# Sums of phi(k) times v in two 64-column halves of the matmul array, two tiles' sums together

## The chip, the cores and the metric

The kernel runs on one core of a Trainium2 chip. The metric is the device time of one execution in microseconds; lower is better. TensorE (PE) multiplies, VectorE (DVE), ScalarE (ACT) and GpSimd (POOL) do the work element by element, and SyncE (SP) issues most DMAs. PEld is the loading of the weights (the stationary operand) of a matmul, which has rows of its own in the profile.

## The reference

```python
# x: (1, 2048, 576); xn = layernorm(x); H = 32 heads of Dh = 18 columns
q, k, v = split(xn @ wqkv)                       # per head
phi = lambda t: jnp.where(t > 0, t + 1, jnp.exp(t)) + 1e-6
pq, pk = phi(q), phi(k)
kv  = einsum("bhsd,bhse->bhde", pk, v)           # the sums: 18 x 18 per head, over all 2048 rows
z   = einsum("bhsd->bhd", pk)
num = einsum("bhqd,bhde->bhqe", pq, kv)
den = einsum("bhqd,bhd->bhq", pq, z)[..., None] + 1e-6
s = (num / den) @ wo
g = silu((gelu(xn @ w_gate) * (xn @ w_up)) @ w_down)   # 576 -> 4608 -> 576
out = x + s * g
```

The change is in `kv` and `z` alone. A head's sum needs only that head's 18 columns of phi(k) against its own 18 columns of v.

## The kernel before

The 2048 rows are 16 tiles of 128 rows (t = 0 to 15). The first part of the program (to about 283 us) makes q, k and v, the sums, and the attention output s; the rest (gate, up and down products with a fast matrix multiplication in blocks) takes the remaining 1180 us and does not change.

**A tile.** `kv_tile(t)` makes k and v of one tile in three products: `x_mm(t, 0)` gives 416 columns of k, `x_mm(t, 1)` the last 160 of k and 252 of v, `x_mm(t, 2)` the last 324 of v and 64 of q. Each is 14 matmuls with operands in fp32r, into one bank of PSUM (`kv_<t>_<c>` in the program; the profile leaves the numbers out and calls all of them `kv`). After `x_mm(t, 0)`, PE broadcasts the next tile's mean and scale (`turn`, tile `ms`; for the first four tiles it transposes x, tile `xt`). DVE forms phi(k) in `pk` (`k_post`: `e_k` and `pk` are its two halves, then ACT takes exp and POOL adds), ACT copies v into `va` (`v_post`), and DVE and ACT normalize and place the next tile (`place`: `x<-x,ms`, `xf_B`, `xo_B`), which the next `x_mm(t + 1, 0)` reads. At the end of each even tile from 2 to 12 DVE takes the moments of two later tiles (`x_next`: `bn`, `mv`, `st`), which a later `turn` broadcasts. All instructions of an engine stand in the order in which the code is written.

**The sums.** `kv_mm(t)` adds tile t's share into PSUM. The 32 heads are five groups: four of 7 heads (126 columns) and one of 4 (72 columns). For each group one fp32 matmul has `va` of the group as weights (a column of ones for z, then 126 or 72 columns of v) and `pk` of the group as the moving operand, so that all 7 x 7 pairs of heads are computed, and the 18 x 18 blocks on the diagonal are cut out by a mask at the end. The groups of 7 lie in the bank `kv_a`, the last in `kv_b`. An fp32 matmul is two matmul instructions and two weight loads in the profile: 4 groups give 8 rows of `kv_a`, the last gives 2 of `kv_b`. `kv_mm(t - 1)` stands in `kv_tile(t)` after `x_mm(t, 2)`; the sums of tiles 0 and 1 stand in tile 2's hand-written code, those of tile 7 and 15 behind the first product of q (`q_store(0, 0)`, `q_hold(2, 7, 0)`). Tile 8 has none.

**Buffers.** `pk` and `va` come from one ring of four (`slot`), so `pk[t]` takes the buffer of `pk[t - 2]`.

**What follows.** `kv_done` multiplies both banks by the mask into `kvm` (DVE). `kv_wo` multiplies `kvm` with the matching rows of `wo` (PE, tile `kw`) into weights that the output product needs. `load_wo` clears row 0 and some columns of `wo_t` and `kvm` on POOL and loads `wo` by DMA. `den` computes the denominators: 5 groups of 4 fp32 matmuls with 32 columns of weights each, the four on the four quarters of the output's partitions (tile `d`).

Of the kernel before, what the change touches and what calls it, by code (L numbers as in the profile page):

```python
# [8 lines left out]
F32 = mybir.dt.float32  # L9
F32R = mybir.dt.float32r  # L10
BF16 = mybir.dt.bfloat16
AF = mybir.ActivationFunctionType
ALU = mybir.AluOpType
# [3 lines left out]
P = 128  # L17
S = 2048
# [12 lines left out]
NHG = 5  # L31
WIDTHS = [GW, GW, GW, GW, D - 4 * GW]
W4 = WIDTHS[4]


Q4 = 64
# [54 lines left out]
def block_kernel(ctx, tc, x, xe, xt, wq_d, wkv_d, wo, wgu_d, wd_d, out):  # L91
# [9 lines left out]
    def own_bank(name):  # L101
        return ps.tile([P, 512], F32, tag="own", bufs=2, name=name)
# [7 lines left out]
    def slot(shape, dt, name):  # L110
        return sb.tile(shape, dt, tag="h", bufs=4, name=name)
# [9 lines left out]
    def act(*args, **kw):  # L121
        pin(nc.scalar.activation(*args, **kw))  # L122

    def vec(op, *args, **kw):
        pin(getattr(nc.vector, op)(*args, **kw))  # L125

    def mm(*args, **kw):
        pin(nc.tensor.matmul(*args, **kw))  # L128

    def pool(op, *args, **kw):  # L130
        pin(getattr(nc.gpsimd, op)(*args, **kw))  # L131

    def dma(out, in_, eng=None):
        tc.keep_in_program_order((eng or nc.sync).dma_start(out=out, in_=in_))
# [156 lines left out]
    def difference(s, i):  # L291
        f = xf[s]
        nm, a, b, o = SUMS[i]
        vec("tensor_sub", f[o], f[a], f[b])
        f[nm] = f[o]
# [81 lines left out]

    acc = []

    def kv_out(gi):  # L380
        return acc[0][:, gi * P : (gi + 1) * P] if gi < 4 else acc[1][:, 0:P]

    def phi(o, src, name):

# [5 lines left out]

    def kv_mm(t):
        if t == 0:
            acc.extend(own_bank(n) for n in ("kv_a", "kv_b"))
        pk, va = pks.pop(t), vas.pop(t)
        for gi, wdt in enumerate(WIDTHS):
            mm(
                kv_out(gi)[0 : wdt + 1, 0:wdt],
                va[:, gi, 0 : wdt + 1], pk[:, gi * GW : gi * GW + wdt],
                start=(t == 0 and gi in (0, 4)), stop=(t == S // P - 1),
                skip_group_check=True,  # L400
            )


    KV_PASSES = [(0, 0), (1, 1), (3, 0), (4, 1), (0, 3), (1, 4), (2, 2)]
# [5 lines left out]
    def x_mm(t, c, js=(0, 1), passes=KV_PASSES):  # L410

        tb, i = divmod(t, TT)
        s, b = divmod(tb, 2)
        begin = (t, c) not in pkv
        if begin:
            pkv[t, c] = bank(f"kv_{t}_{c}")
        o = pkv[t, c]
        for j in js:
            for n, (wi, xi) in enumerate(passes):
                mm(  # L420
                    o[:, 0 : TW[c]], xo[s][BS[b][j]][:, xi, i * P : (i + 1) * P], kv_part(c, j, wi),
                    start=(begin and j == 0 and n == 0), stop=(j == 1 and (wi, xi) == (2, 2)),
                )
# [33 lines left out]
    def v_post(t, c):  # L457

        if c == 1:
            vas[t] = slot([P, NHG, P], F32, f"va_{t}")  # L460
            pool("memset", vas[t][:, :, 0:1], 1.0)
        va, src = vas[t], pkv[t, c]
        n = D - TW[0] if c == 1 else 0
        g = 2 * c - 2
        act(
            va[:, g : g + 2, 1 : GW + 1],
            src[:, n : n + 2 * GW].rearrange("p (g j) -> p g j", g=2), AF.Copy,
        )
        if c == 2:
            act(va[:, 4, 1 : W4 + 1], src[:, 2 * GW : 2 * GW + W4], AF.Copy)  # L470
            tb, i = divmod(t, TT)
            if i == 0:
                qt[tb] = gl_tile([P, TT, 2, Q4], f"qt_{tb}")
            act(
                qt[tb][:, i], src[:, None, 2 * GW + W4 : TW[2]].to_broadcast([P, 2, Q4]), AF.Copy,
            )
# [5 lines left out]
    def kv_tile(t, mid_=(), end=()):  # L482

        ahead = t % (2 * TT) != 2 * TT - 1
        x_mm(t, 0)
        if ahead:
            turn(t + 1)
        k_post(t, 0)
        x_mm(t, 1)
        if ahead:  # L490
            place(t + 1)
            save(t + 1)
        run(list(mid_))
        k_post(t, 1)
        v_post(t, 1)
        x_mm(t, 2)
        if t - 1 in vas:
            kv_mm(t - 1)
        run(list(end))
        v_post(t, 2)  # L500

    ph, ph_d = {}, {}

# [48 lines left out]
    def make_masks():  # L552
        ones = tmp([P, NHG * H], "ones")
        nc.gpsimd.memset(ones, 1.0)

        at["mask"] = mask = small[:, 0:GW]
        m3, o3 = (i.rearrange("p (h j) -> p h j", h=HG) for i in (mask, ones[:, 0:GW]))
        nc.gpsimd.affine_select(
            out=m3, in_=o3, compare_op=ALU.is_ge, fill=0.0, base=-1,
            pattern=[[-DH, HG], [0, DH]], channel_multiplier=1,  # L560
        )
        nc.gpsimd.affine_select(
            out=m3, in_=m3, compare_op=ALU.is_ge, fill=0.0, base=DH,
            pattern=[[DH, HG], [0, DH]], channel_multiplier=-1,
        )
        nc.gpsimd.memset(mask[0:1, :], 1.0)
        at["maskh"] = small[:, P : P + NHG * H].rearrange("p (g h) -> p g h", g=NHG)
        band(at["maskh"], ones.rearrange("p (g h) -> p g h", g=NHG), [[-GW, NHG], [DH, H]], 1)
        at["zc"] = small[:, P + NHG * H : P + 2 * NHG * H].rearrange("p (g h) -> p g h", g=NHG)
        nc.gpsimd.memset(at["zc"][Q4:P], 0.0)  # L570

    def kv_done():

        mask, kvm = at["mask"], at["kvm"]
        n, n4 = GW + 1, W4 + 1
        vec("tensor_mul", kvm[0:n4, 4, 0:W4], acc[1][0:n4, 0:W4], mask[0:n4, 0:W4])
        vec(
            "tensor_mul", kvm[0:n, 0:4, 0:GW],
            acc[0][0:n, :].rearrange("p (g j) -> p g j", g=4)[:, :, 0:GW],
            mask[0:n, None, :].to_broadcast([n, 4, GW]),  # L580
        )

    def load_wo():

        n = NHG * P
        t = big(14, [P, n + D + 2], F32, "kvm")
        at["kvm"] = t[:, 0:n].rearrange("p (g j) -> p g j", g=NHG)
        at["wo"] = w = big(12, [P, 4, D + 2], F32, "wo_t")
        at["wo4"] = w4 = t[:, n:]
        for t in (w, w4[:, None, :]):  # L590
            pool("memset", t[0:1, :, 0:D], 0.0)
            pool("memset", t[:, :, D:], 0.0)
            pool("memset", t[0:1, :, D : D + 1], 1.0)
        dma(out=w[1 : GW + 1, :, 0:D], in_=wo[0 : 4 * GW, :].rearrange("(g p) e -> p g e", p=GW))
        dma(out=w4[1 : W4 + 1, 0:D], in_=wo[4 * GW : D, :])

    def kv_wo(gi):

        if gi == 4:
            at["kvh"] = big(4, [P, 4, D], F32R, "kvh")  # L600
            at["kvl"] = big(5, [P, 4, D], F32R, "kvl")

            at["kv4"] = big(6, [P, 4, D], F32R, "kv4")
            pool("memset", at["kv4"][Q4:P, 1, :].bitcast(F32), 0.0)
        kvh, kvl, kv4 = at["kvh"], at["kvl"], at["kv4"]
        zc, mh = at["zc"], at["maskh"]
        wdt, k = (W4, W4 + 1) if gi == 4 else (GW, GW + 1)
        w = at["wo4"] if gi == 4 else at["wo"][:, gi]
        pw = []
        for c, cs in enumerate((slice(0, HALF), slice(HALF, D + 2))):  # L610
            pw.append(bank(f"kw_{gi}_{c}"))
            mm(
                pw[c][0:wdt, 0 : cs.stop - cs.start], at["kvm"][0:k, gi, 0:wdt], w[0:k, cs],
                start=True, stop=True,
            )
        r, x_ = slice(0, Q4 if gi == 4 else GW), slice(Q4, W4)
        z = pw[1][:, HALF : HALF + 1]

        def parts(hi, lo, rows):
            for c in range(2):  # L620
                cs = slice(c * HALF, (c + 1) * HALF)
                split(hi[:, cs], lo[:, cs], pw[c][rows, 0:HALF])

        if gi == 4:
            vec("tensor_copy", zx[x_], z[x_])
            parts(kv4[x_, 2, :], kv4[x_, 3, :], x_)
            for c in range(2):
                act(kv4[Q4:P, 0, c * HALF : (c + 1) * HALF], pw[c][r, 0:HALF], AF.Copy)

        vec(  # L630
            "tensor_scalar", zc[r, gi, :], mh[r, gi, :], z[r], None, op0=ALU.mult,
        )
        if gi == 4:
            parts(kv4[r, 0, :], kv4[r, 1, :], r)
        else:
            parts(kvh[r, gi, :], kvl[r, gi, :], r)
# [754 lines left out]
    for passes in (HI_X, LO_X):  # L1391
        for j in range(2):
            x_mm(2, 0, (j,), passes)
    kv_mm(0)
    turn(3)
    k_post(2, 0)
    x_mm(2, 1)
# [3 lines left out]
    k_post(2, 1)  # L1401
    v_post(2, 1)
    x_mm(2, 2)
    kv_mm(1)
    x_next(4)
    v_post(2, 2)
    load_q(0)
# [27 lines left out]
    def form_apart(nm):  # L1435
# [11 lines left out]
        dma(out=d[:, 2], in_=last[:, 0].bitcast(F32))  # L1447

    behind = {
        (0, 0): [lambda: kv_mm(N0 - 1), lambda: spread(N0, 2), lambda: difference(0, 3)],  # L1450
        (0, 1): [
            lambda: scales(N0), lambda: form("T1"), lambda: q_store(1, 4),
        ],
# [9 lines left out]
    for n in range(N0, 2 * N0):  # L1463
# [12 lines left out]
        if n in (N0, N0 + 2):  # L1476
            load_x(n + 4, 2)
    ahead = {
        (2, 0): [lambda: kv_mm(2 * N0 - 1), kv_done, spread_sel, lambda: difference(1, 3)],
        (2, 1): [lambda: kv_wo(4), lambda: q_hold(2, 7, 4)],  # L1480
        (2, 2): [lambda: kv_wo(0), lambda: kv_wo(1), move_rows],
        (2, 3): [lambda: kv_wo(2), lambda: kv_wo(3)],
# [118 lines left out]
```

## Time and profile before

| | before |
|---|---|
| time, median of 3 runs | 1461.74 us (1460.86 to 1463.02) |
| the profiled execution | 1461.7 us, span 1460.0 us |
| granted TensorE clock | 1.00 |
| PE busy | 1452.8 us, 100% of the span |
| DVE busy | 1154.8 us, 79% |
| `kv_a` matmuls | 128 rows, 16.7 us busy |
| `kv_b` matmuls | 32 rows, 4.7 us busy |

The profiled execution took 1.7 us more than its span. A row of the timeline gives the start in us from the span's beginning, the length in us, the engine, the line, the operation, the tiles (written <- read), the sizes, and how many instructions are merged; brackets hold the idle time of the engine before it and what ended it. A matmul's length contains the way through the array, so that matmuls in a row overlap: the step from start to start is what one costs.

### The profile page before, as it was taken

Reading aid. Unit: us, or ns where it says so; the run is one execution under the profiler, and the core shown is the slowest. Engines: PE = TensorE matmul, PEld = TensorE weight load, DVE = VectorE, ACT = ScalarE, POOL = GpSimd, SP = SyncE. Lnnn points to the kernel's source line nnn. Section 1 sums busy time; section 2 is a strip of 40 time slices with the busy share of each in tenths; the row PEclk is TensorE's granted clock in tenths of the full one; section 3 lists DMA queues with packets and bytes.
Section 4 is the critical chain, followed back from the end, with each engine's and each line's share of the span. In section 5 each row is a group of like instructions: output and inputs, shape, how many; then the busy total and the mean of one; then the engine's idle time right before and its main releaser. Section 6 shows DMA issues by size and latency. Waiting matters only on the chain.

```text
span 1460.0 us, 21848 instructions
## 1 busy us (share of the span) xinstructions
PE 1452.8 (100%) x8126; PEld 1297.1 (89%) x8126; DVE 1154.8 (79%) x1603; ACT 561.5 (38%) x914; POOL 577.9 (40%) x512
## 2 busy tenths in 40 slices
PE   9999999999999999999999999999999999999998
PEld 8989989988888888888888888888889999999998
DVE  7687676376888787878778878778788978989888
ACT  6344265333222332322333222322335556555454
POOL 3342340125665567565575664657632000000000
PEclk9999999999999999999999999999999999999999
DMA  6445006531333315323152242323379888767886
GB/s 228 164 188 194 6 2 214 192 144 57 124 123 115 129 58 174 101 94 130 61 178 87 94 152 84 133 87 106 130 268 354 268 259 250 251 187 234 276 291 223
DMA packets 118068, 233.96 MB, mean 160 GB/s; under 512 B 11002, under 2 KB 44666, under 8 KB 116042
## 3 DMA queue, kind: packets, MB, share of 16 engines
q1 hardware_dynamic: 115162, 220.31, 45.0%
q0 software_dynamic: 2656, 12.06, 2.2%
q8 instruction: 64, 1.05, 0.3%
q14 instruction: 42, 0.34, 0.1%
q10 hardware_dynamic: 144, 0.20, 0.0%
HBM read 149.91 MB, written 82.58 MB: 159 GB/s over the span
## 4 chain that ended last, share of the span: by engine, by line
PE 97%; DVE 2%; ACT 0%; issue 0%; DMA 0%; DVEq 0%; ACTq 0%
PE bd L128 25%; PE ga L818 16%; PE de L818 16%; PE al L818 16%; PE be L818 8%; PE kv L128 8%; PE s L128 4%; PE q L128 4%; PE kv_a L128 1%; PE d L128 0%; PE kw L128 0%; PE b L128 0%; DMA x<-in_xe_dram 0%; DVE acc L125 0%; PE xt L221 0%
## 5 line engine op out<-in xcount | busy, mean ns | idle before, releaser
L131 POOL TENSOR_TENSOR sm<-raw 128x384 f32<-128x384 f32 x72 | 75.5, 1049 | 148.8 <-DMA raw<-in_wgu_dram 113.8
L128 PE MATMUL kv<-wkv,xo_B 128*128 128x412 f32 (+2 forms) x662 | 128.0, 349 | 0.0
L125 DVE TENSOR_TENSOR wa<-sm,wa 128x768 fp32r<-128x768 f32 x72 | 94.7, 1315 | 36.1 <-ACT wa L122 35.3
L128 PEld LDWEIGHTS kv<-wkv,xo_B 128*128 128x128 f32 x662 | 119.6, 188 | 1.0 <-ACT xo_B L122 0.2
L128 PE MATMUL bd<-w_head,hi 128*128 128x288 f32 x516 | 117.9, 294 | 0.0
L125 DVE TENSOR_TENSOR wb<-raw,wb 128x256 fp32r<-128x256 f32 (+1 forms) x108 | 103.9, 962 | 7.4 <-ACT wb L122 5.8
L125 DVE TENSOR_TENSOR wa<-raw,wa 128x256 fp32r<-128x256 f32 x72 | 68.7, 955 | 51.0 <-ACT wa L122 47.7
L122 ACT ACTIVATE hi<-raw_h 128x1024 fp32r<-128x1024 f32 x59 | 62.4, 1060 | 94.2 <-PE bd L128 60.8
L128 PE MATMUL bd<-w_end,hi 128*128 128x288 f32 x448 | 89.8, 294 | 0.0
L122 ACT ACTIVATE spot_h<-spot_h 128x512 f32<-128x512 f32 x49 | 30.8, 633 | 152.0 <-DVE spot_h L125 152.0
L128 PEld LDWEIGHTS bd<-w_head,hi 128*128 128x128 f32 x516 | 87.0, 188 | 0.1
L125 DVE TENSOR_TENSOR raw_h<-raw_h,hi 128x1024 fp32r<-128x1024 f32 x59 | 71.7, 1219 | 18.5 <-ACT hi L122 18.5
L128 PE MATMUL bd<-w_end,raw_h 128*128 128x288 f32 x264 | 77.9, 295 | 0.0
L122 ACT ACTIVATE wa<-sm 128x1152 fp32r<-128x1152 f32 x36 | 41.8, 1161 | 88.5 <-PE de L818 86.3
L122 ACT ACTIVATE u<-al 128x512 f32<-128x512 f32 x72 | 41.0, 593 | 89.7 <-PE al L818 69.0
L128 PEld LDWEIGHTS bd<-w_end,hi 128*128 128x128 f32 x448 | 71.9, 188 | 0.0
L128 PE MATMUL bd<-beside,raw_h 128*128 128x288 f32 x240 | 70.8, 295 | 0.0
L131 POOL TENSOR_TENSOR spot_h<-spot_h,spot_h 128x512 f32<-128x512 f32 x45 | 62.8, 1401 | 2.9 <-DVE spot_h L125 2.4
L818 PE MATMUL ga<-xo_B,wb 128*128 128x512 f32 x252 | 63.1, 390 | 0.4 <-DVE u L125 0.4
L818 PE MATMUL al<-xo_B,wa 128*128 128x512 f32 x252 | 63.0, 389 | 0.0
L818 PE MATMUL al<-xr_B,wa 128*128 128x512 f32 x252 | 63.0, 389 | 0.0
L818 PE MATMUL be<-xr_T,wa 128*128 128x512 f32 x252 | 63.0, 389 | 0.0
(274 smaller groups left out, 4055.1 us busy)
## 6 DMA issues: line engine op xcount, KB each, us to landing
raw_h<-hs SPq DMA_DIRECT2D x176, 256.0 KB
raw<-in_wgu_dram SPq DMA_DIRECT2D x36, 768.0 KB
hs<-spot_h SPq DMA_DIRECT2D x90, 256.0 KB
hs<-spot_g SPq DMA_DIRECT2D x80, 256.0 KB
b<-in_wd_dram SPq DMA_DIRECT2D x42, 432.0 KB
hs<-spot_m SPq DMA_DIRECT2D x38, 256.0 KB
raw_g<-hs SPq DMA_DIRECT2D x22, 256.0 KB
raw_a<-hs SPq DMA_DIRECT2D x20, 256.0 KB
```

Source lines behind the costliest of these rows:

```text
L122: pin(nc.scalar.activation(*args, **kw))
L125: pin(getattr(nc.vector, op)(*args, **kw))
L128: pin(nc.tensor.matmul(*args, **kw))
L131: pin(getattr(nc.gpsimd, op)(*args, **kw))
L818: nc.tensor.matmul(o, w[0:rows, wi, :], xop[0:rows, xi, :], start=(start and n == 0), stop=(n == len(PASSES) - 1), skip_group_check=True,)
```

## The change

Each group is now two matmuls on two halves of the array's columns. The first half has the ones and the group's first 63 columns of v (3.5 heads) as weights and writes to partitions 0 to 63, the second the ones and the other 63 to partitions 64 to 127. The middle head is split between them. Against each go only the 4 heads of phi(k) that its half touches (72 columns instead of 126). The group of 4 heads becomes two halves of 37 weights and 36 moving columns. All lie in the one bank `kv_a`. `va` has ten pieces of 64 columns instead of five of 128. And the sums of two tiles are made one after the other: `kv_pair(t)` stands in even tiles behind `x_mm(t, 0)`, ahead of `turn`, and makes tiles t - 2 and t - 1; the pairs for 6 and 7, and for 14 and 15, stand behind the first product of q.

```diff
+KC = 4 * DH
-    def kv_out(gi):
-        return acc[0][:, gi * P : (gi + 1) * P] if gi < 4 else acc[1][:, 0:P]
+    def kv_out(gi, half):
+        n, m = (KC, GW // 2) if gi < 4 else (W4 // 2, W4 // 2)
+        c = half * ((GW if gi < 4 else W4) - n)
+        r = half * P // 2
+        return acc[0][r : r + m + 1, gi * KC : gi * KC + n], slice(c, c + n)
...
         for gi, wdt in enumerate(WIDTHS):
-            mm(
-                kv_out(gi)[0 : wdt + 1, 0:wdt],
-                va[:, gi, 0 : wdt + 1], pk[:, gi * GW : gi * GW + wdt],
-                start=(t == 0 and gi in (0, 4)), stop=(t == S // P - 1),
+            for half in range(2):
+                o, cs = kv_out(gi, half)
+                mm(
+                    o, va[:, 2 * gi + half, 0 : o.shape[0]],
+                    pk[:, gi * GW + cs.start : gi * GW + cs.stop],
+                    start=(t == 0 and gi == 0), stop=(t == S // P - 1),
...
 def v_post(t, c):
-            va[:, g : g + 2, 1 : GW + 1],
-            src[:, n : n + 2 * GW].rearrange("p (g j) -> p g j", g=2), AF.Copy,
+            va[:, g : g + 4, 1 : GW // 2 + 1],
+            src[:, n : n + 2 * GW].rearrange("p (g j) -> p g j", g=4), AF.Copy,
...
 def kv_tile(t, mid_=(), end=()):
         x_mm(t, 0)
+        if t % 2 == 0:
+            kv_pair(t)
         if ahead:
             turn(t + 1)
...
         x_mm(t, 2)
-        if t - 1 in vas:
-            kv_mm(t - 1)
+    def kv_pair(t):
+        for i in (t - 2, t - 1):
+            if i in vas:
+                kv_mm(i)
...
 def kv_done():          # two multiplications by a mask become four, two for each half
-        vec("tensor_mul", kvm[0:n4, 4, 0:W4], acc[1][0:n4, 0:W4], mask[0:n4, 0:W4])
+            vec("tensor_mul", kvm[r, 4, cs], o, mask[r, 0 : W4 // 2])
+            vec(
+                "tensor_mul", kvm[r, 0:4, cs],
+                acc[0][r, 0 : 4 * KC].rearrange("p (g j) -> p g j", g=4),
+                at["mask"][r, None, :].to_broadcast([P // 2, 4, KC]),
+            )
...
 def load_wo():          # wo's rows lie in two halves too; what no row covers is zero
+        pool("memset", at["kvm"], 0.0)
         for t in (w, w4[:, None, :]):
-            pool("memset", t[0:1, :, 0:D], 0.0)
-            pool("memset", t[:, :, D:], 0.0)
-            pool("memset", t[0:1, :, D : D + 1], 1.0)
-        dma(out=w[1 : GW + 1, :, 0:D], in_=wo[0 : 4 * GW, :].rearrange("(g p) e -> p g e", p=GW))
-        dma(out=w4[1 : W4 + 1, 0:D], in_=wo[4 * GW : D, :])
+            pool("memset", t, 0.0)
+            for r in (0, P // 2):
+                pool("memset", t[r : r + 1, :, D : D + 1], 1.0)
+        for half in range(2):
+            r = half * P // 2 + 1
...
+            dma(out=w[r : r + n, :, 0:D], in_=rows[:, half])
...
+            dma(out=w4[r : r + n, 0:D], in_=wo[f : f + n, :])
```

`make_masks` builds the masks of the two halves in six steps on POOL instead of two, with four short memsets instead of one, and `kv_wo` sums over 128 and 101 rows instead of 127 and 73.

The order on PE around tile 10, where `pk_1193` and `va_1225` belong to tile 8 and `pk_1268` and `va_1300` to tile 9; first as it stood before, from the last matmul of tile 9's products to the broadcast for tile 11:

```order
L128 MATMUL kv_2_1303<-wkv_73,xo_B_1079 128x388
L128 MATMUL kv_a<-pk_1193,va_1225 127x126 x4
L128 MATMUL kv_b<-pk_1193,va_1225 73x72
L128 MATMUL kv_0_1332<-wkv_71,xo_B_1076 128x416 x7
L128 MATMUL kv_0_1332<-wkv_72,xo_B_1079 128x416 x7
L213 MATMUL ms_1347<-ident,mv_1117 128x128
L213 MATMUL ms_1347<-ident,st_1124 128x128
L128 MATMUL kv_1_1354<-wkv_73,xo_B_1076 128x412 x7
```

The same place now (the buffers of tiles 8 and 9 are `pk_1239`, `va_1271` and `pk_1314`, `va_1346`):

```order
L129 MATMUL kv_2_1349<-wkv_73,xo_B_1125 128x388
L129 MATMUL kv_0_1373<-wkv_71,xo_B_1122 128x416 x7
L129 MATMUL kv_0_1373<-wkv_72,xo_B_1125 128x416 x7
L129 MATMUL kv_a<-pk_1239,va_1271 64x72 x8
L129 MATMUL kv_a<-pk_1239,va_1271 37x36 x2
L129 MATMUL kv_a<-pk_1314,va_1346 64x72 x8
L129 MATMUL kv_a<-pk_1314,va_1346 37x36 x2
L214 MATMUL ms_1408<-ident,mv_1163 128x128
L214 MATMUL ms_1408<-ident,st_1170 128x128
```

The sum of tile 8 has moved behind the first product of tile 10, that of tile 9 from behind tile 10's last product to the same place, and the broadcast `ms` for tile 11 comes behind both.

On POOL at the end of tile 13 stood, between the last addition of phi(k) of that tile and the next, these rows of `load_wo`:

```order
L131 TENSOR_TENSOR pk_1616<-pk_1616,e_k_1617 128x576
L131 MEMSET va_1648 128x5
L131 MEMSET wo_t 1x4x576
L131 MEMSET wo_t 128x4x2
L131 MEMSET wo_t 1x4
L131 MEMSET kvm 1x576
L131 MEMSET kvm 128x2
L131 MEMSET kvm 1x1
L131 TENSOR_TENSOR pk_1702<-pk_1702,e_k_1703 128x576
```

Now there stand:

```order
L132 TENSOR_TENSOR pk_1682<-pk_1682,e_k_1683 128x576
L132 MEMSET va_1714 128x10
L132 MEMSET kvm 128x640
L132 MEMSET wo_t 128x2312
L132 MEMSET wo_t 1x4 x2
L132 MEMSET kvm 128x578
L132 MEMSET kvm 1x1 x2
L132 TENSOR_TENSOR pk_1786<-pk_1786,e_k_1787 128x576
```

The memsets clear whole tiles instead of one row and two columns, and the DMAs that fill `wo_t` and `kvm` write over what they cleared.

More of the change, by code (lines that the diff above doesn't have):

```diff
@@ L392, in kv_mm @@
         if t == 0:
-            acc.extend(own_bank(n) for n in ("kv_a", "kv_b"))
+            acc.append(own_bank("kv_a"))
         pk, va = pks.pop(t), vas.pop(t)
         for gi, wdt in enumerate(WIDTHS):
-            mm(
-                kv_out(gi)[0 : wdt + 1, 0:wdt],
-                va[:, gi, 0 : wdt + 1], pk[:, gi * GW : gi * GW + wdt],
-                start=(t == 0 and gi in (0, 4)), stop=(t == S // P - 1),
-                skip_group_check=True,
-            )
+            for half in range(2):
[4 more added lines that the diff above has]
+                    start=(t == 0 and gi == 0), stop=(t == S // P - 1),
+                    skip_group_check=True,
+                )
     KV_PASSES = [(0, 0), (1, 1), (3, 0), (4, 1), (0, 3), (1, 4), (2, 2)]
@@ L459, in v_post @@
         if c == 1:
-            vas[t] = slot([P, NHG, P], F32, f"va_{t}")
+            vas[t] = slot([P, 2 * NHG, P // 2], F32, f"va_{t}")
             pool("memset", vas[t][:, :, 0:1], 1.0)
@@ L463, in v_post @@
         n = D - TW[0] if c == 1 else 0
-        g = 2 * c - 2
+        g = 4 * c - 4
         act(
-            va[:, g : g + 2, 1 : GW + 1],
-            src[:, n : n + 2 * GW].rearrange("p (g j) -> p g j", g=2), AF.Copy,
+            va[:, g : g + 4, 1 : GW // 2 + 1],
+            src[:, n : n + 2 * GW].rearrange("p (g j) -> p g j", g=4), AF.Copy,
         )
         if c == 2:
-            act(va[:, 4, 1 : W4 + 1], src[:, 2 * GW : 2 * GW + W4], AF.Copy)
+            act(
+                va[:, 8:10, 1 : W4 // 2 + 1],
+                src[:, 2 * GW : 2 * GW + W4].rearrange("p (g j) -> p g j", g=2), AF.Copy,
+            )
             tb, i = divmod(t, TT)
@@ L554, in make_masks, with blocks @@
         nc.gpsimd.memset(ones, 1.0)
[L556 to L565, printed above, removed]
+        at["mask"] = mask = small[:, 0:KC]
+        at["mask4"] = mask4 = small[:, KC : KC + W4 // 2]
+        low, high = slice(0, P // 2), slice(P // 2, P)
+        def blocks(m, rows, nh, first):
+            v = m[rows].rearrange("p (h j) -> p h j", h=nh)
+            o = ones[rows, 0 : nh * DH].rearrange("p (h j) -> p h j", h=nh)
+            nc.gpsimd.affine_select(
+                out=v, in_=o, compare_op=ALU.is_ge, fill=0.0, base=first - 1,
+                pattern=[[-DH, nh], [0, DH]], channel_multiplier=1,
+            )
+            nc.gpsimd.affine_select(
+                out=v, in_=v, compare_op=ALU.is_ge, fill=0.0, base=DH - first,
+                pattern=[[DH, nh], [0, DH]], channel_multiplier=-1,
+            )
+        blocks(mask, low, 4, 0)
+        blocks(mask, high, 4, GW // 2 - 3 * DH)
+        blocks(mask4, high, 2, 0)
         nc.gpsimd.memset(mask[0:1, :], 1.0)
+        nc.gpsimd.memset(mask[P // 2 : P // 2 + 1, 0:DH], 0.0)
+        nc.gpsimd.memset(mask[P // 2 : P // 2 + 1, DH:], 1.0)
+        nc.gpsimd.memset(mask4[P // 2 : P // 2 + 1, :], 1.0)
         at["maskh"] = small[:, P : P + NHG * H].rearrange("p (g h) -> p g h", g=NHG)
@@ L572, in kv_done @@
     def kv_done():
-        mask, kvm = at["mask"], at["kvm"]
-        n, n4 = GW + 1, W4 + 1
-        vec("tensor_mul", kvm[0:n4, 4, 0:W4], acc[1][0:n4, 0:W4], mask[0:n4, 0:W4])
[L577 to L581, printed above, removed]
+        kvm = at["kvm"]
+        for half, mask in enumerate((at["mask"], at["mask4"])):
+            o, cs = kv_out(4, half)
+            n = o.shape[0]
+            r = slice(half * P // 2, half * P // 2 + n)
+            vec("tensor_mul", kvm[r, 4, cs], o, mask[r, 0 : W4 // 2])
+        for half in range(2):
+            _, cs = kv_out(0, half)
+            r = slice(half * P // 2, (half + 1) * P // 2)
+            vec(
+                "tensor_mul", kvm[r, 0:4, cs],
+                acc[0][r, 0 : 4 * KC].rearrange("p (g j) -> p g j", g=4),
+                at["mask"][r, None, :].to_broadcast([P // 2, 4, KC]),
+            )
     def load_wo():
@@ L589, in load_wo @@
         at["wo4"] = w4 = t[:, n:]
+        pool("memset", at["kvm"], 0.0)
         for t in (w, w4[:, None, :]):
-            pool("memset", t[0:1, :, 0:D], 0.0)
-            pool("memset", t[:, :, D:], 0.0)
-            pool("memset", t[0:1, :, D : D + 1], 1.0)
-        dma(out=w[1 : GW + 1, :, 0:D], in_=wo[0 : 4 * GW, :].rearrange("(g p) e -> p g e", p=GW))
-        dma(out=w4[1 : W4 + 1, 0:D], in_=wo[4 * GW : D, :])
+            pool("memset", t, 0.0)
+            for r in (0, P // 2):
+                pool("memset", t[r : r + 1, :, D : D + 1], 1.0)
+        for half in range(2):
+            r = half * P // 2 + 1
+            n = GW // 2
+            rows = wo[0 : 4 * GW, :].rearrange("(g h p) e -> p h g e", h=2, p=n)
+            dma(out=w[r : r + n, :, 0:D], in_=rows[:, half])
+            n = W4 // 2
+            f = 4 * GW + half * n
+            dma(out=w4[r : r + n, 0:D], in_=wo[f : f + n, :])
     def kv_wo(gi):
@@ L606, in kv_wo @@
         zc, mh = at["zc"], at["maskh"]
-        wdt, k = (W4, W4 + 1) if gi == 4 else (GW, GW + 1)
+        wdt, k = (W4, P // 2 + W4 // 2 + 1) if gi == 4 else (GW, P)
         w = at["wo4"] if gi == 4 else at["wo"][:, gi]
@@ L1393, in block_kernel @@
             x_mm(2, 0, (j,), passes)
-    kv_mm(0)
+    kv_pair(2)
     turn(3)
@@ L1403, in block_kernel @@
     x_mm(2, 2)
-    kv_mm(1)
     x_next(4)
@@ L1449, in block_kernel @@
     behind = {
-        (0, 0): [lambda: kv_mm(N0 - 1), lambda: spread(N0, 2), lambda: difference(0, 3)],
+        (0, 0): [lambda: kv_pair(N0), lambda: spread(N0, 2), lambda: difference(0, 3)],
         (0, 1): [
@@ L1478, in block_kernel @@
     ahead = {
-        (2, 0): [lambda: kv_mm(2 * N0 - 1), kv_done, spread_sel, lambda: difference(1, 3)],
+        (2, 0): [lambda: kv_pair(2 * N0), kv_done, spread_sel, lambda: difference(1, 3)],
         (2, 1): [lambda: kv_wo(4), lambda: q_hold(2, 7, 4)],
```

## The prediction

> **What bounds the kernel now.** First the page's chain and PE's waits over the whole program:
>
> ```profile
> PE 97%; DVE 2%; ACT 0%; issue 0%; DMA 0%; DVEq 0%; ACTq 0%
> PE ga L818 <- DVE u L125: 0.4, 1, 0.4
> ```
>
> The chain that ended last is PE at 97%, and the only wait of PE behind the start that this view lists is 0.4 us, far behind the change. So a microsecond of PE time saved in the sums is a microsecond of the program, as long as the other engines keep up there. Next the sums themselves, loads and matmuls by tile, then PE's timeline at tile 5's end and at tile 2:
>
> ```profile
> L128 PEld LDWEIGHTS kv_a<-pk,va x128: 186/191/191, 28.8 to 184.2; 128*127 128x127 f32 x128
> L128 PE MATMUL kv_a<-pk,va x128: 268/274/274, 29.0 to 184.3; 128*127 128x126 f32 x128
> L128 PEld LDWEIGHTS kv_b<-pk,va x32: 144/145/146, 29.8 to 184.4; 128*73 128x73 f32 x32
> L128 PE MATMUL kv_b<-pk,va x32: 226/228/229, 29.9 to 184.5; 128*73 128x72 f32 x32
> ```
>
> ```profile
> 63.18 1.04 PE L128 MATMUL kv_a<-pk,va 128*127 128x126 f32 x8
> 64.06 0.29 PE L128 MATMUL kv_b<-pk,va 128*73 128x72 f32 x2
> 64.16 2.90 PE L128 MATMUL kv<-wkv,xo_B 128*128 128x416 f32 x14
> ...
> 109.29 2.80 PE L128 MATMUL kv<-wkv,xo_B 128*128 128x416 f32 x14
> ```
>
> ```profile
> 29.02 1.05 PE L128 MATMUL kv_a<-pk,va 128*127 128x126 f32 x8
> 29.91 0.29 PE L128 MATMUL kv_b<-pk,va 128*73 128x72 f32 x2
> 30.04 0.82 PE L221 MATMUL xt<-ident,x 128*128 128x128 f32 x6
> ```
>
> Steps from start to start: `kv_a` (1.04 - 0.274) / 7 = 0.109 us for 126 moving columns, `kv_b` 0.29 - 0.228 = 0.062 us for 72. A tile's sums take 64.16 - 63.18 = 0.98 us, and the fp32r product behind them takes 2.90 instead of 2.80 us (the row at 109.29 has no sums ahead of it): 0.10 us more, at its first matmul. So 1.08 us for each of 14 tiles. Two are followed by fp32 transposes instead; the one shown took 30.04 - 29.02 = 1.02. Together 14 x 1.08 + 2 x 1.02 = 17.2 us.
>
> **What two halves cost.** No row has matmuls of 64 weight columns. The nearest are the denominators, four quarters of 32 columns each, between two products of q:
>
> ```profile
> L128 PEld LDWEIGHTS d<-ph,small x160: 106/110/110, 202.8 to 255.2; 128*32 128x32 f32 x160
> L128 PE MATMUL d<-ph,small x160: 272/273/297, 202.8 to 255.3; 128*32 128x128 f32 x160
> ```
>
> ```profile
> 202.53 0.39 PE L128 MATMUL q<-xo_B,wq 128*128 128x512 f32 x1
> 202.84 1.30 PE L128 MATMUL d<-ph,small 128*32 128x128 f32 x40
> 204.07 0.66 PE L510 MATMUL q<-ident,qt 128*128 128x128 f32 x4
> ```
>
> Their step is (1.30 - 0.273) / 39 = 0.026 us, while an fp32 matmul of 128 columns over the whole array steps by (0.82 - 0.274) / 5 = 0.109 (the six `xt`). So four quarters run at once, loads included, each at its own 0.105 us. I take the same for two halves. Loads: 110, 145 and 191 ns for 32, 73 and 127 columns make 0.85 ns a column, so 0.054 us for 64 columns and 0.031 for 37, on top of a fixed part that overlaps. Both are no longer than the matmuls beside them (0.062 for 72 moving columns, half of it, 0.031, for 36; I take 0.033 for the short ones).
>
> One tile, each half: 8 x 0.062 + 2 x 0.033 = 0.56 us, the other half beside it. A pair of tiles 1.12, with 0.04 for the second half's later end 1.16. The row of d bounds it below: 40 matmuls at 0.026 are 1.04; halves that take turns bound it above (a rival).
>
> Going in and out costs. The last q starts at 202.53; products of q step by 0.22 (28 in 6.36 in the chain's row below), so d could start at 202.75 and does at 202.84: 0.09 to 0.10. Its last matmul starts at 204.14 - 0.27 = 203.87, streams 0.11, and the next begins at 204.07: 0.09. Then the first transpose is 0.06 late (0.66 - 0.273 - 3 x 0.109), the weights that nothing hid.
>
> ```profile
> 90.16 6.36 PE q L128 x28
> ```
>
> A pair therefore: in 0.10 plus an unhidden load 0.054, body 1.16, out 0.09 + 0.06, together 1.46 us. Two of the eight pairs are followed by q, with a load of 128 columns, 0.11 instead of 0.06. Sum: 8 x 1.46 + 0.1 = 11.8 us, against 17.2: **5.4 us less of PE work.** Making two tiles together halves the entries and exits; single tiles would pay 0.31 eight times more.
>
> The Trainium skill warns here, in "TensorE: Matmul & The Clock Gate", section "The mechanism": a weight load overlaps running matmuls only when it goes to another group of rows. Both halves use all rows, so by that rule no load would be hidden; its time is among the rivals. The d rows speak against it, as they keep 0.105 us a round with all rows in use.
>
> **Where the gain is lost: tile 11.** The rows are DVE's, then PE's:
>
> ```profile
> 120.11 0.59 DVE L125 TENSOR_SCALAR e_k<-kv 128x416 f32<-128x416 f32 x1 [1.05 <-PE kv L128]
> ...
> 127.68 1.92 DVE L125 TENSOR_TENSOR xo_T<-xf_B,xo_T 128x1024 fp32r<-128x1024 f32 x2 [2.22 <-ACT xo_T L122]
> ...
> 137.99 0.16 DVE L125 SCALAR_TENSOR_TENSOR st<-st 128x2 f32<-128x2 f32 x1
> ```
>
> ```profile
> 119.84 0.27 PE L213 MATMUL ms<-ident,mv 128*128 128x128 f32 x1
> ...
> 125.17 1.04 PE L128 MATMUL kv_a<-pk,va 128*127 128x126 f32 x8
> ...
> 137.85 0.27 PE L213 MATMUL ms<-ident,mv 128*128 128x128 f32 x1
> 138.21 0.32 PE L213 MATMUL ms<-ident,st 128*128 128x128 f32 x1
> ```
>
> In tile 9 ACT and DVE build T4 (`xo_T`), and DVE runs from the first product of tile 9 (120.11) to the scales of tile 12 (137.99 + 0.16 = 138.15) with waits on ACT alone. PE already waits there: `ms` of `st` starts 0.36 instead of 0.11 behind `ms` of `mv`. Between 119.84 and 137.85 lie two single sums (2.16); one pair (1.46) would bring PE there 0.70 us sooner, to wait for the same 138.15. So the pair of tiles 8 and 9 gives nothing: 5.4 - 0.7 = 4.7.
>
> **The other covers.** With the sum gone from an odd tile's end, x_mm(10, 0) can start at 125.17. It reads `xo_B`, finished by DVE at
>
> ```profile
> 123.36 1.51 DVE L125 TENSOR_TENSOR xo_B<-xf_B,xo_B 128x256 fp32r<-128x256 f32 x4
> ```
>
> that is 124.87, 0.3 us before, in the tile where DVE is latest. The pair needs phi(k) and v of the newer tile, which before had a whole tile's time; now they must be there some 2.7 + 0.15 + 0.56 us behind 125.17, at 128.6:
>
> ```profile
> 126.08 1.43 POOL L131 TENSOR_TENSOR pk<-pk,e_k 128x576 f32<-128x576 f32 x1 [4.93 <-ACT e_k L122]
> 127.55 0.49 ACT L122 ACTIVATE va<-kv 128x252 f32<-128x252 f32 x2
> ```
>
> They end at 127.51 and 128.04. Copying v in four pieces instead of two costs ACT an unknown amount, from nothing to once more the copy (0.36); I take nothing, 0.6 us of slack cover it. In even tiles DVE now must wait for the pair's first tile before it may write `pk`, as it did once in tile 2:
>
> ```profile
> 30.31 0.59 DVE L125 TENSOR_SCALAR pk<-kv 128x416 f32<-128x416 f32 x1 [0.36 <-PE kv_b L128]
> ```
>
> Behind it stands `place`, which waits for `ms` anyway, and that now comes after the pair. Tile 12 shows what that does:
>
> ```profile
> 147.25 0.27 PE L213 MATMUL ms<-ident,st 128*128 128x128 f32 x1
> ...
> 156.28 0.27 PE L213 MATMUL ms<-ident,st 128*128 128x128 f32 x1
> ```
>
> ```profile
> 148.47 0.95 DVE L125 TENSOR_TENSOR x<-x,ms 128x768 f32<-128x768 f32 x1
> ...
> 155.71 0.16 DVE L125 SCALAR_TENSOR_TENSOR st<-st 128x2 f32<-128x2 f32 x1
> ```
>
> `ms` would end at 147.52 + 1.46 = 148.98, so `place` starts about 0.55 later, the scales of tile 14 end at 156.4, and PE wants them at 156.28 + 1.46 - 1.08 = 156.66: no wait, by 0.25 us.
>
> `load_wo` clears whole tiles, and its DMAs now wait for that:
>
> ```profile
> 163.62 2.20 POOL L131 MEMSET wo_t<- 1x2304 f32 x3
> 165.80 0.75 POOL L131 MEMSET kvm<- 1x576 f32 x3
> ```
>
> By columns (3,530 against some 2,900 in 2.95 us) that is 3.6 us, done near 167; `kw` reads it only behind the last sums, which begin at 184.3 (the `kv_a` row); behind those DMAs SP has nothing due. The four mask multiplications of `kv_done` take at most four times the longest of before (0.67 us in the row below), 2.7 us, under the product of q that PE makes between; I take nothing. The masks are made in the first microseconds, where POOL idles 3.76 us on ACT. All nothing.
>
> ```profile
> L125 DVE TENSOR_TENSOR kvm<-kv_a,small x1: 669/669/669, 185.1 to 185.1; 127x504 f32<-127x504 f32 x1
> ```
>
> ```profile
> 6.91 3.09 POOL L131 TENSOR_TENSOR wkv<-rw,wkv 128x832 fp32r<-128x832 f32 x2 [3.76 <-ACT wkv L122]
> ```
>
> The profiled execution took 1461.7 us (span 1460.0), as the median of the runs did (1461.74). 1461.7 - 4.7 = **1457.0**.
>
> **The rivals.**
> *Halves take turns* (slower). If matmuls of the two halves do not run at once, a tile is 16 x 0.062 + 4 x 0.033 = 1.12, a pair 2.25 + 0.31 = 2.56, eight of them 20.6 with the 0.1: 3.4 us more than 17.2, so 1465.1. It decides from a body of 1.84 us a pair, where 8 x (1.84 + 0.31) reaches 17.2. For it: no 64-column row exists. Against: the 0.026 of d. Chance 0.11.
> *Loads wait for the matmuls in their rows.* Halves run at once, but each step is 0.054 + 0.062: a tile 8 x 0.116 + 2 x 0.064 = 1.06, a pair 2.12 + 0.31 = 2.43, together 19.5: 1464.0. Chance 0.04. This is what the Trainium skill's rule on row groups, named above, would make of it.
> *DVE becomes the bound* in the even tiles, as in tile 11: three margins of 0.25 to 0.6 us were found; if they fail and five of eight pairs give nothing, 3 x 0.67 = 2.0 us remain: 1459.7. Chance 0.10.
> *The gain is given back later*, the one wait for `u` growing by it: 1461.7. Chance 0.03.
>
> **How the numbers follow.** The forecast has 0.72. Its own range: body at 1.04 and entries as cheap as loads alone (0.2) give 8 x 1.24 = 9.9, seven eighths of 7.3 saved: 1455.3; entries and exits twice as dear (0.31 more a pair, 2.2 over seven) give 1459.2. A measurement of this kernel tells about 0.2%, 2.9 us, from no change. Faster means below 1458.8: nearly all of the forecast and a little of DVE's case, 0.69. Slower, above 1464.7: halves in turns, 0.12. Between: 0.19. The range for eight in ten is the forecast's own with the DVE case: 1455.3 to 1460.6.
>
> **What would show it.** Right: 256 `kv_a` matmuls of 72 columns and 64 of 36; forty in about 1.4 us from first start to last end (1.16 + 0.23 of length), the next matmul some 0.1 us behind the stream's end; the first product behind `ms` no later; PE's wait at tile 11's `ms` grown to about 1 us. Wrong: a pair of over 2 us, or waits of PE for `st`, `xo_B`, `pk` or `va` in other tiles.

## The result and the profile after

| | before | after |
|---|---|---|
| time, median of 7 runs each | 1461.76 us | 1456.91 us (1456.15 to 1457.43) |
| ratio | | 0.9966, 95% interval 0.9954 to 0.9978 |
| profiled span | 1460.0 us | 1454.9 us |
| first denominator matmul (`d`) starts | 202.84 us | 198.21 us |

The kernel became 4.85 us faster; 1457.0 had been forecast. Of the 5.1 us between the two spans, 4.63 are there at the first denominator, where everything that the change touches is done. The other half microsecond lies behind, in the part that does not change: the 0.4 us wait of `ga` for `u` that the page of before had is not in this profile.

The tile `kv_a` after the change (loads, matmuls, the multiplications by the mask), and of what follows, who waited for it:

```profile
L129 PEld LDWEIGHTS kv_a<-pk,va x320: 112/136/139, 29.1 to 179.7; 128*64 128x64 f32 x128, 128*37 128x37 f32 x32
L129 PE MATMUL kv_a<-pk,va x320: 193/224/278, 29.1 to 179.7; 128*64 128x72 f32 x128, 128*37 128x36 f32 x32
L126 DVE TENSOR_TENSOR kvm<-kv_a,small x4: 176/324/461, 180.5 to 181.4; 37x36 f32<-37x36 f32 x2, 64x288 f32<-64x288 f32 x2
...
  DVE pk L126: 0.8, 4
```

There are twice as many matmuls as before, each of 72 or 36 moving columns (the forms in this row are a sample of half of them). PE's timeline from tile 8 to tile 12, where each pair of `ms` is the broadcast for the next tile:

```profile
109.25 0.27 PE L214 MATMUL ms<-ident,mv 128*128 128x128 f32 x1
109.36 0.27 PE L214 MATMUL ms<-ident,st 128*128 128x128 f32 x1
109.39 7.94 PE L129 MATMUL kv<-wkv,xo_B 128*128 128x412 f32 x42
117.17 0.27 PE L214 MATMUL ms<-ident,mv 128*128 128x128 f32 x1
117.28 0.27 PE L214 MATMUL ms<-ident,st 128*128 128x128 f32 x1
117.31 7.99 PE L129 MATMUL kv<-wkv,xo_B 128*128 128x412 f32 x42
125.23 1.38 PE L129 MATMUL kv_a<-pk,va 128*64 128x72 f32 x40
126.55 0.32 PE L214 MATMUL ms<-ident,mv 128*128 128x128 f32 x1
126.71 0.27 PE L214 MATMUL ms<-ident,st 128*128 128x128 f32 x1
126.73 7.95 PE L129 MATMUL kv<-wkv,xo_B 128*128 128x412 f32 x42
134.52 0.27 PE L214 MATMUL ms<-ident,mv 128*128 128x128 f32 x1
135.56 0.32 PE L214 MATMUL ms<-ident,st 128*128 128x128 f32 x1 [0.77 <-DVE st L126]
```

The distance of two `ms` is the cleanest measure of a tile. Without sums it is 117.17 - 109.25 = 7.92 us in tile 8. The tiles are not all alike without sums: tile 9 takes 7.97 (125.99 - 118.02 in the run with the broadcast ahead of the pair, below), because the starts of its second product's matmuls span 2.32 us instead of 2.27. And a pair's cost does not end at the broadcast: behind a pair, `st` starts 0.16 us behind `mv` instead of 0.11 (126.71 and 126.55). So tiles 9 and 10 are taken together. Without sums they take 7.97 + 7.92 = 15.89 us; here, from 117.17 to 134.52, they take 17.35, so a pair costs 1.46 us. Before, with two single sums, the same two tiles took 18.01:

```profile
119.84 0.27 PE L213 MATMUL ms<-ident,mv 128*128 128x128 f32 x1
...
128.86 0.27 PE L213 MATMUL ms<-ident,mv 128*128 128x128 f32 x1
...
137.85 0.27 PE L213 MATMUL ms<-ident,mv 128*128 128x128 f32 x1
```

That is 2.12 for two sums, 1.06 for one. And in tile 11 the second broadcast now starts 135.56 - 134.52 = 1.04 us behind the first, where 0.36 was the distance before and 0.11 is the distance without a wait: the gain of the pair of tiles 8 and 9 is lost there.

### The profile page after: what moved, and what is told of

Its sections match the earlier page's. It is cut to its first block, busy times and chain, and to the rows that moved or that the text cites. A ratio compares the mean times of both kernels' runs of the same rounds, so it can differ in the third digit from the quotient of the medians.

```text
span 1454.9 us, 22180 instructions
## 1 busy us (share of the span) xinstructions
PE 1447.7 (100%) x8286; PEld 1290.2 (89%) x8286; DVE 1152.8 (79%) x1605; ACT 562.5 (39%) x914; POOL 579.1 (40%) x520
## 3 DMA queue, kind: packets, MB, share of 16 engines
q8 instruction: 65, 1.06, 0.3%
## 4 chain that ended last, share of the span: by engine, by line
PE 94%; DVE 3%; DMA 2%; issue 0%; ACT 0%; SPq 0%; POOL 0%; DVEq 0%; ACTq 0%; POOLq 0%
PE bd L129 21%; PE al L859 16%; PE de L859 16%; PE ga L859 16%; PE kv L129 8%; PE be L859 8%; PE s L129 4%; PE q L129 4%; DMA raw_h<-hs 1%; DVE sx L126 1%; PE kv_a L129 1%; DMA sx<-in_x_dram 0%; DVE raw_h L126 0%; DVE acc L126 0%; PE idle L129 0%
## 5 line engine op out<-in xcount | busy, mean ns | idle before, releaser
L859 PE MATMUL be<-xo_T,wa 128*128 128x512 f32 x252 | 63.0, 389 | 0.0
```

The costliest lines, as they stand in the source:

```text
L859: nc.tensor.matmul(o, w[0:rows, wi, :], xop[0:rows, xi, :], start=(start and n == 0), stop=(n == len(PASSES) - 1), skip_group_check=True,)
```

## The experiments

In all of them the distance of the two `ms` around tiles 9 and 10 gives a pair (or two single sums) as the excess over 15.89 us. The ratios are to runs of before in the same rounds. There before took 1461.59 us beside the first four experiments and 1461.13 beside the last two.

| kernel | time, median (us) | one pair, or two sums (us) | `ms` to `ms` in tile 11 |
|---|---|---|---|
| before | 1461.76 | 2 x 1.06 | 0.36 |
| after | 1456.91 | 1.46 | 1.04 |
| halves, single tiles | 1459.83 | 2 x 0.91 | 0.66 |
| pairs over the whole array | 1461.37 | 2.08 | 0.40 |
| both halves on the same columns | 1465.54 | 2.60 | 0.11 |
| after, T4 on POOL | 1455.98 | 1.46 | 0.11 |
| the same, broadcast ahead of the pair | 1456.97 | 1.55 | 0.11 |
| before, T4 on POOL | 1461.02 | 2 x 1.06 | 0.11 |

**The halves without the pairs.** `kv_mm` stands where it stood before:

```diff
         x_mm(t, 0)
-        if t % 2 == 0:
-            kv_pair(t)
...
         x_mm(t, 2)
+        if t - 1 in vas:
+            kv_mm(t - 1)
```

> The two halves, but each tile's sums where they stood before, one tile at a time. Theory (halves run at once, each entry or exit of the column mode costs what it did around the denominators): a tile costs 0.10 + 0.054 in, 0.58 of matmuls, 0.09 + 0.11 out, 0.93 us instead of 1.08, two tiles 0.88 instead of 1.02. That is 2.4 us less than before; 0.3 of it is lost to the wait at tile 11. The first denominator starts near 200.7 us (before 202.84, after 198.21), the time is about 1459.7. Rival (the gain comes from moving and pairing the sums, not from the halves): no gain against before, 1461.8 or more.

Measured: 1459.83 us (1458.72 to 1460.68), ratio to before 0.9986 (0.9977 to 0.9995). PE's timeline, at tiles 9 and 10:

```profile
120.21 0.27 PE L214 MATMUL ms<-ident,mv 128*128 128x128 f32 x1
...
125.63 0.79 PE L129 MATMUL kv_a<-pk,va 128*64 128x72 f32 x20
126.35 2.90 PE L129 MATMUL kv<-wkv,xo_B 128*128 128x416 f32 x14
129.08 0.27 PE L214 MATMUL ms<-ident,mv 128*128 128x128 f32 x1
...
137.92 0.27 PE L214 MATMUL ms<-ident,mv 128*128 128x128 f32 x1
138.58 0.32 PE L214 MATMUL ms<-ident,st 128*128 128x128 f32 x1 [0.38 <-DVE st L126]
```

The two tiles take 137.92 - 120.21 = 17.71 us, 1.82 for two sums and 0.91 for one; 0.93 had been worked out. A pair takes 1.46: one entry and exit less is worth 0.36. The halves alone bring some 1.8 us (1461.59 to 1459.83); the rest of the 4.85 comes from pairing them. The first denominator came at 202.38 and not at 200.7, but in this profile PE reached the first `ms` (40.70) 1.2 us later than before (39.50), waiting 0.9 us for `xf_B` at the start. Why was not looked into, and the eleven times, spread over 2 us, do not tell whether other executions had this wait.

**The pairs without the halves.** The code of before, with `kv_pair` behind `x_mm(t, 0)` as in the change.

> The sums over the whole array as before, but two tiles together behind the first product of even tiles. Theory: a tile's sums are 0.98 us as before, and what goes is only the 0.10 us on the way back from fp32 to fp32r matmuls, since the broadcast behind the pair pays it anyway: 16 x 0.98 + 2 x 0.10 = 15.9 us instead of 17.2, 1.3 less, of which 0.2 are lost at tile 11. First denominator near 201.7, time about 1460.7. Rival (pairing is where most of the 4.85 us came from): near 1457 to 1458.

Measured: 1461.37 us, ratio 0.9998 (0.9989 to 1.0007): no difference that can be told. The rival falls, and PE's timeline shows that the theory's price was wrong too:

```profile
119.63 0.27 PE L213 MATMUL ms<-ident,mv 128*128 128x128 f32 x1
...
127.60 1.05 PE L128 MATMUL kv_a<-pk,va 128*127 128x126 f32 x8
128.48 0.29 PE L128 MATMUL kv_b<-pk,va 128*73 128x72 f32 x2
128.61 1.09 PE L128 MATMUL kv_a<-pk,va 128*127 128x126 f32 x8
129.54 0.29 PE L128 MATMUL kv_b<-pk,va 128*73 128x72 f32 x2
129.67 0.27 PE L213 MATMUL ms<-ident,mv 128*128 128x128 f32 x1
...
137.60 0.27 PE L213 MATMUL ms<-ident,mv 128*128 128x128 f32 x1
```

The pair costs 137.60 - 119.63 - 15.89 = 2.08 us, 0.04 less than two single sums (2.12), where the theory had 0.20 less. So the 0.10 us that a tile's sums seemed to charge to the product behind them is not a price of going back to fp32r, which a broadcast behind the pair would pay anyway. About half of it is a load: the next matmul's 127 or 128 columns (0.109 us) do not fit under the last short matmul (0.062), and the second tile's sum pays this just so (1.09 against 1.05 for its eight matmuls). The broadcast does not pay it, because its loads, with `ident`, are shorter (0.13 to 0.14 us, where those of `kv_a` take 0.19); that accounts for the 0.04:

```profile
L213 PEld LDWEIGHTS ms<-ident,mv x12: 133/134/140, 39.2 to 165.9; 128*128 128x128 f32 x12
```

Most of the rest is in the records: the product's first matmul is recorded 0.03 us behind the start of the last short one, which alone steps by 0.062, and looks longer by as much. So pairing is worth little where there is no entry into the column mode (the array split into halves) to save.

**Both halves on the same 64 columns.** The second half writes to partitions 0 to 63 of a second bank; loads, matmuls and columns are as many.

```diff
-        return acc[0][r : r + m + 1, gi * KC : gi * KC + n], slice(c, c + n)
+        return acc[half][0 : m + 1, gi * KC : gi * KC + n], slice(c, c + n)
```

> As changed, but both halves of every group use the same 64 columns of the array (and two banks), so that nothing runs at once; instructions, loads and columns are the same in number. Theory: a tile's matmuls take 16 x 0.062 + 4 x 0.033 = 1.12 us instead of 0.57, 16 tiles 8.8 us more, of which the wait at tile 11 hides 0.9: first denominator near 206.1, time about 1464.8. Rival (the gain came from fewer moving columns per matmul and not from halves at once): 1457, as changed.

Measured: 1465.54 us (1464.63 to 1465.85), ratio to before 1.0027 (1.0017 to 1.0037). One group after the other in PE's timeline:

```profile
122.19 0.27 PE L214 MATMUL ms<-ident,mv 128*128 128x128 f32 x1
...
130.56 0.29 PE L129 MATMUL kv_a<-pk,va 128*64 128x72 f32 x2
130.68 0.29 PE L129 MATMUL kv_b<-pk,va 128*64 128x72 f32 x2
130.81 0.29 PE L129 MATMUL kv_a<-pk,va 128*64 128x72 f32 x2
...
132.72 0.32 PE L214 MATMUL ms<-ident,mv 128*128 128x128 f32 x1
...
140.68 0.27 PE L214 MATMUL ms<-ident,mv 128*128 128x128 f32 x1
```

Each matmul of the two in a row steps by some 0.062 us, 0.125 from one half to the next, and a pair takes 140.68 - 122.19 - 15.89 = 2.60 us (2.56 worked out). With the same 0.31 for going in and out, the matmuls take 2.29 there and 1.15 in the change: two halves on different columns run at once, in full. This is the shown cause of the gain. It is also the rival "halves take turns", 1465.1 on paper, made real.

**T4 on POOL.** The two subtractions at the end of T4, in tile 9, by `pool` instead of `vec`:

```diff
-            ends.append(lambda: form("T4"))
+            ends.append(lambda: form("T4", pool))
```

> As changed, but the two subtractions that end T4 in tile 9 run on POOL instead of DVE. Theory (the wait of PE for the scales of tile 12 comes from DVE, which T4 delays): DVE is 1.9 us and a wait of 2.2 us on ACT earlier, the second broadcast of tile 11 follows 0.11 us behind the first instead of 1.04, first denominator near 197.3, time about 1456.0. Rival (another wait stands right behind it, POOL's slower subtraction or its pressure on DVE's transfers): the wait shrinks by less than half, time 1456.6 or more.

Measured: 1455.98 us (1455.6 to 1456.99), ratio to before 0.9962 (0.995 to 0.9975). POOL's rows, then PE's:

```profile
125.33 3.73 POOL L132 TENSOR_TENSOR xo_T<-xf_B,xo_T 128x1024 fp32r<-128x1024 f32 x2 [0.15 <-ACT xo_T L123]
```

```profile
117.44 0.27 PE L214 MATMUL ms<-ident,mv 128*128 128x128 f32 x1
...
134.79 0.27 PE L214 MATMUL ms<-ident,mv 128*128 128x128 f32 x1
134.90 0.27 PE L214 MATMUL ms<-ident,st 128*128 128x128 f32 x1
```

The subtractions take 3.73 us on POOL instead of 1.92 on DVE, in time in which POOL had nothing to do, and the wait is gone: 0.11 us. It was DVE's, and the edit returns it: from the first `ms` (tile 3) to the first denominator 158.49 us instead of 159.42, 0.93 less, as the medians are (though the intervals of the two ratios overlap). Its median is the lowest of the study.

**The broadcast ahead of the pair**, on top of that:

```diff
-        if t % 2 == 0:
-            kv_pair(t)
         if ahead:
             turn(t + 1)
+        if t % 2 == 0:
+            kv_pair(t)
```

> T4 on POOL as in the run before, and in even tiles the broadcast of the next tile's mean and scale stands ahead of the pair instead of behind it. Theory: the way out of the pair then leads straight to an fp32r product, 0.09 + 0.11 us instead of 0.09 + 0.06, but the 0.10 us from the fp32 broadcast to that product is gone: 0.05 us less in each of six or seven pairs, 0.3 us in all, about 1455.7; DVE gets the broadcast 1.4 us sooner in even tiles, where PE no longer waits for it. Rival (the way from column mode to fp32r costs both, 0.09 and 0.10): 0.4 us more, about 1456.4.

Measured: 1456.97 us (1456.44 to 1458.12), ratio to before 0.9971 (0.9961 to 0.9982): 1.0 us more than with the broadcast behind the pair, though the intervals of the two ratios overlap.

```profile
118.02 0.27 PE L214 MATMUL ms<-ident,mv 128*128 128x128 f32 x1
...
125.99 0.27 PE L214 MATMUL ms<-ident,mv 128*128 128x128 f32 x1
126.10 0.27 PE L214 MATMUL ms<-ident,st 128*128 128x128 f32 x1
126.30 1.38 PE L129 MATMUL kv_a<-pk,va 128*64 128x72 f32 x40
...
135.46 0.27 PE L214 MATMUL ms<-ident,mv 128*128 128x128 f32 x1
```

A pair takes 135.46 - 118.02 - 15.89 = 1.55 us, 0.09 more. The entry costs the same from a broadcast as from a product (126.10 + 0.11 to 126.30, 0.09). The exit shows the longer load: the second matmul behind the pair is 0.10 us late, where behind a broadcast it was 0.05. And the 0.10 that should have gone was never there: the same misreading as in the pairs without the halves. The other 0.05 of the 0.09 lies in the second product of tile 10, which takes 2.32 us here instead of 2.27; why was not looked into. From the first `ms` to the first denominator the loss is 0.55 us (159.04 against 158.49). The two profiles lie 1.4 us apart in all: 0.3 ahead of the first `ms`, and 0.5 behind the denominator, where `ga` waits 0.4 us for `u` in this profile and not in the other.

**T4 on POOL in the kernel before.**

> The kernel before with T4's subtractions on POOL alone. Theory: PE's second broadcast of tile 11 waited 0.25 us there, against 0.93 in the changed kernel, so the same edit is worth 0.25 us here, about 1461.4, and 0.11 us from broadcast to broadcast. Rival (the edit helps by itself, through DVE's time elsewhere): as much as in the changed kernel, 0.9 us, about 1460.7.

Measured: 1461.02 us, ratio to before 0.9999 (0.999 to 1.0008). The time cannot tell the two theories apart (0.9 us would be a ratio of 0.9994); the trace can:

```profile
119.79 0.27 PE L213 MATMUL ms<-ident,mv 128*128 128x128 f32 x1
...
137.80 0.27 PE L213 MATMUL ms<-ident,mv 128*128 128x128 f32 x1
137.91 0.27 PE L213 MATMUL ms<-ident,st 128*128 128x128 f32 x1
```

0.11 instead of 0.36, and from the first `ms` to the first denominator 163.00 us instead of 163.34. The wait was worth a quarter of a microsecond before the change and nearly four times that after it.

## Why the prediction was right

- **Two halves at once.** 0.56 us a tile beside each other was worked out from the denominators' four quarters. A pair takes 1.46 us, as forecast, and twice the matmul time when the halves share columns.
- **In and out.** The forecast was 0.10 plus a load of 64 columns in, and 0.09 plus a load out. Going in took 0.09 and 0.045, going out 0.10 and 0.05 (0.10 where q follows). The step from 1.46 for a pair to 2 x 0.91 for single tiles is 0.36, against 2 x 0.93 - 1.46 = 0.40 on paper. About half of it is loads that nothing hides.
- **A term that no row gave.** The 0.04 for the second half's later end was not read from any row, and the runs do not show it: the second half follows within 0.01 us. What filled its place is 0.03 us at the second tile's first load, which the sum did not have. That the 1.46 came out to the hundredth is luck in this part.
- **The sum.** 5.4 us of PE work less was the forecast. By the distances of `ms`, 14 x 1.06 + 2 x 1.02 = 16.9 before and 8 x 1.46 + 0.1 = 11.8 after: 5.1. At the first denominator 4.63 of it were left, where 4.7 had been forecast. That the time itself came within 0.1 us of the forecast is in part luck, as half a microsecond between the two profiles lies where the forecast had nothing.
- **Tile 11.** A wait of 0.36 + 0.70 was forecast between the two broadcasts, 1.04 was measured, and taking T4 from DVE returned 0.93 us. This term was the difference between 1456.3 and 1457.0.
- **The rule on row groups** from the Trainium skill, "TensorE: Matmul & The Clock Gate", section "The mechanism" (a load overlaps running matmuls only in another group of rows; or, as the section also says, into a background buffer for weights), does not hold here by its rows alone: both halves use all of them. With no load hidden a pair would take 2.43 us, as the prediction worked out, and it takes 1.46. Whether the loads go through such a buffer, the runs do not show.
- **The covers held.** `va` in four pieces takes what it took in two (median 363 ns in both profiles). DVE waited for the pair before writing `pk` four times, 0.8 us in all, without PE waiting in turn. `load_wo`'s memsets end at 164.06, at 3.8 us instead of 3.6. The four multiplications by the mask were in time for `kw`, which follows the product of q without a gap. The rows are those of `va`, of the last memset on POOL and of `kw` on PE in the changed kernel:

```profile
L123 ACT ACTIVATE va<-kv x48: 225/363/383, 22.0 to 175.7; 128x252 f32<-128x252 f32 x32, 128x72 f32<-128x72 f32 x16
```

```profile
163.20 0.86 POOL L132 MEMSET kvm<- 128x578 f32 x3
```

```profile
182.92 0.39 PE L129 MATMUL q<-xo_B,wq 128*128 128x512 f32 x1
183.15 1.14 PE L129 MATMUL kw<-kvm 101*72 101x288 f32 x4
```

- **What was misread.** The 0.10 us behind a tile's sums was about right as a part of 1.08 (1.06 measured), but not as a price of the way back to fp32r. In the change itself little hung on it; two experiments built on it missed.
- **What stays open.** The wait of `ga` for `u`, about half a microsecond, is in the profiles of before, of the last two experiments (0.4 and 0.2 us there), and in none of the others; the pairs over the whole array have one of 0.7 us of `bd` for `raw_h` instead. Whether the change moved it, or it comes and goes, was not settled; it is within what the forecast's range allowed.

## What to carry to other kernels

Where a block-diagonal product wastes most of a full-width matmul, two halves of the array's columns with fewer moving columns each can run at once, weights included, as they did here, and rows of other column-tiled matmuls in the same trace gave a good price for them. What must be counted beside it is each entry and exit, 0.3 to 0.4 us together with the loads that nothing hides, so such matmuls should stand together. And a gain on the bounding engine should be followed to the next place where it waits for another: here one tile took back an eighth of it, and moving one small step to an idle engine returned that.

## What the runs showed of the hardware

- fp32 matmuls of 64 weight columns in two halves: a step of 0.062 us for 72 moving columns in each half, the second half's within 0.01 us of the first's; on the same columns the two take 0.125 us.
- A change between the whole array and columns cost 0.09 to 0.10 us each way in which nothing starts, plus the first load: 0.045 us for 64 columns on the way in, on the way out 0.05 to an fp32 broadcast and 0.10 to an fp32r product. The way in was the same from an fp32r product and from an fp32 broadcast. Sums over the whole array in the same place (the pairs without the halves) show no such gap.
- Loads of 128 columns are not all alike: those with `ident` for the broadcasts are recorded with 0.13 to 0.14 us, those of the products with 0.19.
- The recorded start of a product's first matmul behind a short matmul can be early: behind `st` of tile 10 it starts after 0.03 us and the next one 0.27 later, where 0.11 and 0.19 are the usual steps, 0.30 both ways. The row looks as if the matmul had taken longer, and the missing time belongs to what came before. The step from start to start over the whole stage is the safer measure.
